# Splitting the feature fetch, splitting the second fork, and a new hand-written order in a convolution and SwiGLU kernel

## The chip, the cores and the metric

The kernel runs on one core of a Trainium2 chip. The metric is the device time of one execution in microseconds (us). Three executions of the kernel before gave 2668.44, 2670.3 and 2671.73 us; their median, 2670.3 us, is the time before. The engines are named as in the profile: PE is TensorE (its matmuls), PEld its weight loads, DVE is VectorE, ACT is ScalarE, POOL is GpSimd, and SP is SyncE, which here issues nearly all DMAs.

## The reference

A causal convolution with seven taps per head, an RMS norm, and a SwiGLU feed-forward block, all in float32:

```python
# x (8, 4096, 192), weight (8 heads, 7 taps)
w = softmax(weight, axis=-1)
out[b, s, h, g] = sum_k w[h, k] * x_pad[b, s + k, h, g]     # 6 zeros ahead of each sequence
# tokens: x = out.reshape(32768, 192)
xn = x / sqrt(mean(x * x, axis=-1) + 1e-6) * rms_g
g, val = xn @ w_gate, xn @ w_val                            # 192 -> 1536, each
return (silu(g) * val) @ w_out                              # 1536 -> 192
```

The weights come as float64 words and are converted on the chip once, at the start.

## The kernel before

**Tiling.** The 32768 tokens are handled as 32 pairs of 1024 tokens; a pair is two groups of T = 512. Pair 0 is computed by a plain method during the start of the kernel. Pairs 1 to 31 run in one loop and use fast matrix multiplication (sums of operands in place of some products), so that PE has fewer products to do and the other engines have more additions. The profile's steady state is this loop.

**One pair on PE.** A generator, `Pair.products`, gives 204 steps. Steps 0 to 119 are the products (L732): four units (`Unit`, a unit is 3 of the 12 blocks of 128 hidden features), each with the 15 entries of `CHAIN`, and each entry for the two halves h = 0 (gate, PE rows 0 to 63) and h = 1 (value, rows 64 to 127). They add into six values per half, held in the PSUM banks `ps`, of which there are four for each half. Steps 120 to 203 are the output products (L862): 42 times a wide and a slim step, in the nine runs of `OUTS`. In this text the product stage is steps 0 to 119 of a pair, the output stage is steps 120 to 203.

**Operands of the products.** `xb` holds the pair's features, six blocks of 64 x 512 (twice, for the two halves of PE's rows): x0 to x2 are group 0 and x3 to x5 are group 1. `xc` holds ten sums of them, written by `x_sum` (L655). Both have a single buffer. `XSUM` names the sums: X0 = x1 + x4, X3 = x3 + x5, X8 = x0 + x1 and X9 = x1 + x2 read `xb` alone, X1, X2, X4, X6 and X7 read `xb` and an earlier sum, X5 and X10 two earlier sums. The first products of a pair read X6 (step 0), X10 (step 2), X5 (step 6).

**The order.** `ORDER` is a hand-written string. A token `pN` lets PE's program go on by N steps; any other token is an engine letter (A = ACT, V = DVE, G = POOL, D = SP) and one action. A token with a minus belongs to the pair before. So the string fixes each engine's queue, and semaphores that the framework adds from the data fix the rest: each engine takes its queue in order. The actions that the text uses:

- `Sk.h.u` copies a PSUM bank into an SBUF tile, `C`, `D`, `R` add such a tile and a bank (DVE, L748 to L756), `G` is the SiLU (ACT, L769), `M` the product of gate and value (L776).
- `F0`, `F2`, `F3` are the forks (L693 to L697): a bank is copied into another bank, and both then go on as separate sums. `F2.h.u` copies the bank of value 4 after step 18 + h of the unit (counted from 0), and step 22 + h of the same unit adds into the bank that was copied, so it waits for the copy.
- `cvK_j` is tap K of the convolution of the pair after the next, in three parts j (tap 0 on ACT, the rest on DVE, L445); `sq`, `red`, `pow`, `bc`, `mul` are its RMS norm. 
- `S1.k` to `S4.k` are the sums of hidden blocks that the output products read (POOL, L890).
- `c1`, `s7`, `c2`, `C22`, `C21` (L908) combine the output banks X, Y, Z, and `T11` to `T22` (L877) transpose them into the output tile. `C22` reads bank X between step 179, the last one of a run of `OUTS`, and step 186, which adds into X again. The next pair's step 0 takes the bank that `T12` has read last, and its step 1 the one that `C21` has read last.
- `Dplace` writes normalised features to DRAM (`xd`), `Dfetch` reads the next pair's features back into `xb`, `Dload` loads x for the pair three on, `Dst0` and `Dst1` store the output.

`fetch` issues four DMAs of 384 KB on SP's queue, group 1 first. They may begin when the pair's last product has read `xb`.

Of the kernel before, what the change touches and what calls it, by code (L numbers as in the profile page):

```python
# [11 lines left out]
F32 = mybir.dt.float32  # L12
# [7 lines left out]
def kernel(  # L20
# [10 lines left out]
    nc = tc.nc  # L31
# [11 lines left out]
    T = 512  # L43
# [3 lines left out]
    HP = P // 2  # L47
# [10 lines left out]
    LOW, UPP = slice(0, HP), slice(HP, P)  # L58
# [29 lines left out]

    SPAN = 1509
    ORDER = (  # L90
        "p2 VT21- p2 AS40.1.0 VT11- GX4- AS40.0.0 p2 Vbc- AF0.0.0 Gmul- AF0.1.0 p2 Dst1-",
        "VC.0.0 Dst0- p2 VC.1.0 AS41.1.0 AS41.0.0 p2 AS00.1.0 AS00.0.0 p2 VD5.1.0 p2 VD5.0.0",
        "AS42.0.0 VS42.1.0 AS51.0.0 Dplace- p2 AS51.1.0 VR1.0.0 p2 VR1.1.0 VR0.0.0 p2 AF2.0.0",
        "VR0.1.0 AF2.1.0 p1 AF3.0.0 VF3.1.0 p2 AS44.0.0 p1 AG0.0.0 VR5.0.0 p1 AS44.1.0 p1",
        "GM0.1.0 VR2.0.0 p1 VR2.1.0 AG2.0.0 p2 VR5.1.0 AG4.0.0 GM2.1.0 p1 VR3.1.0 p1 AS40.0.1",
        "VR3.0.0 p1 AS40.1.1 p1 VM4.1.0 AF0.0.1 p1 AF0.1.1 p1 VC.0.1 AG3.0.0 p2 VC.1.1",
        "AS41.0.1 GM3.1.0 p1 AG5.0.0 p1 AS41.1.1 p1 GM5.1.0 VS00.1.1 AS00.0.1 p2 VD5.0.1 p1",
        "GS3.0 AS42.0.1 VD5.1.1 p1 AS42.1.1 p1 VR1.0.1 AS51.0.1 p1 GS3.1 AG1.0.0 p1 VR1.1.1",
        "AS51.1.1 p1 VR0.1.1 p1 GS1.0 AF2.0.1 p1 VR0.0.1 AF2.1.1 p1 AF3.0.1 p1 GS2.0 AF3.1.1",
        "p1 VS44.0.1 AG1.0.1 p2 AS44.1.1 VR5.0.1 GM1.1.1 p1 VR2.1.1 p1 AG5.0.1 p1 VR2.0.1 p1",  # L100
        "AG4.0.1 VR3.1.1 p1 AG0.0.1 p1 VR5.1.1 AS40.0.2 p1 GM0.1.1 VR3.0.1 p1 AS40.1.2",
        "VM4.1.1 p1 AF0.0.2 p1 GM1.1.0 AF0.1.2 VC.0.2 p1 AG3.0.1 p1 VC.1.2 p1 GM3.1.1",
        "VS41.0.2 p1 AS00.0.2 VS41.1.2 p1 AS00.1.2 p1 VM5.1.1 AG2.0.1 p1 GS1.1 VD5.0.2 p1",
        "AS42.0.2 VD5.1.2 p1 AS51.0.2 p1 GS3.2 VR1.0.2 AS42.1.2 p1 AS51.1.2 p1 VR1.1.2 p1",
        "GM2.1.1 VR0.0.2 p1 AF2.0.2 VR0.1.2 p1 AF2.1.2 p1 VF3.0.2 AG1.0.2 p1 VF3.1.2 p1",
        "GM1.1.2 AS44.0.2 p1 AG0.0.2 VR5.0.2 p1 AS44.1.2 GS1.2 p1 VR2.0.2 p1 VR2.1.2 AG2.0.2",
        "p1 GS2.1 p1 VR3.1.2 AG4.0.2 p1 VR3.0.2 p1 AS40.0.3 GM2.1.2 VR5.1.2 p1 AS40.1.3 p1",
        "VM4.1.2 AF0.0.3 p1 GM0.1.2 AG3.0.2 p1 VC.0.3 AF0.1.3 p2 VC.1.3 AG5.0.2 GM3.1.2 p1",
        "VS41.0.3 p1 AS00.0.3 VS41.1.3 p1 GM5.1.2 AS00.1.3 p1 VD5.0.3 p2 VD5.1.3 GS2.2",
        "AS42.0.3 p1 AS51.0.3 p1 VR1.0.3 AS42.1.3 GS3.3 p1 AS51.1.3 p1 VR1.1.3 p1 VR0.0.3",  # L110
        "GS3.4 p1 VF2.0.3 p1 AF2.1.3 VR0.1.3 AG0.0.3 p2 VF3.0.3 AF3.1.3 GM0.1.3 p2 AS44.1.3",
        "AS44.0.3 p1 GS1.3 p1 VR2.0.3 AG1.0.3 p1 VR2.1.3 p1 GM1.1.3 VR3.0.3 Acv0_1 p1 VR3.1.3",
        "AG3.0.3 p2 GS2.3 VR5.1.3 AG4.0.3 p2 Acv0_2 VM4.1.3 Dfetch p1 Acv0_0 p1 VM3.1.3 p1",
        "AG2.0.3 p1 GS3.5 Vcv1_1 p2 VR5.0.3 p2 GS1.4 Vcv1_2 AG5.0.3 p2 Ac1 p1 VM5.1.3 p2",
        "GS2.4 Vcv2_1 p2 Vcv2_2 p2 GS1.5 Vcv1_0 p2 Vcv3_1 p1 As7 GS4.2 p2 Vcv4_1 p2 Vcv2_0",
        "GS2.5 p2 Vcv5_1 p2 GS4.1 Vcv6_1 p2 Vcv3_0 p2 GM2.1.3 Vcv3_2 p3 Vcv4_2 p1 GS4.0 p2",
        "Vcv5_2 Ac2 p2 GX0 Vcv4_0 p2 Vcv6_2 p1 GS4.3 p1 Vcv5_0 p2 Vcv6_0 p2 VX1 p1 Asq p1 VX8",
        "p2 VX9 p1 Dload p1 VX3 p2 VC22 p2 VX6 p2 GS4.4 Vred p3 GS4.5 p4 VX5 p2 VX2 p1 VX7 p2",
        "VX10 p2 Gpow VT12 p2 VT22 p2 VC21 p1",
    )  # L120

    cst = ctx.enter_context(tc.tile_pool(name="cst", bufs=1))
# [5 lines left out]
    dram = ctx.enter_context(tc.tile_pool(name="dram", bufs=2, space=bass.MemoryType.DRAM))  # L128
# [109 lines left out]
    def load_out(i):  # L238
# [28 lines left out]
        out=taps[:], in0=w_sb[:], in1=stat[:].to_broadcast([P, H, K]), op=ALU.subtract  # L267
# [7 lines left out]
        out=taps[:], in0=taps[:], in1=ssum[:].to_broadcast([P, H, K]), op=ALU.mult  # L275
# [51 lines left out]
    xb = cst.tile([P, 2, KP, T], F32, name="xb")  # L327
# [46 lines left out]
    scr = {}  # L374
# [261 lines left out]
    def x_op(i):  # L636
        return xb[:, i // KP, i % KP, :] if i < 2 * KP else xc[:, i - 2 * KP, :]

    def fetch(p):

        if p >= PAIRS:
            return
        xd = scr.pop(p)
        for g in (1, 0):
            for rows in (LOW, UPP):
                nc.sync.dma_start(
                    out=xb[rows, g],
                    in_=xd[:, g * T : (g + 1) * T].rearrange("(k p) t -> p k t", p=HP),
                )

    def x_sum(i, eng="V"):

        d, a, b = XSUM[i]
        e = nc.gpsimd if eng == "G" else nc.vector
        e.tensor_tensor(out=xc[:, d, :], in0=x_op(a), in1=x_op(b), op=ALU.add)  # L655
# [23 lines left out]
    def put(at, do):  # L679
        heapq.heappush(line, (at, next(tick), do))  # L680
# [5 lines left out]
    def plus(s):  # L686
        return ALU.add if s > 0 else ALU.subtract
# [3 lines left out]
    def copy(eng, dst, src, s=1):  # L691
        if eng == "A":
            nc.scalar.activation(out=dst, in_=src, func=AF.Copy, scale=float(s))  # L693
        elif s < 0:
            nc.vector.tensor_scalar(out=dst, in0=src, scalar1=-1.0, scalar2=None, op0=ALU.mult)
        else:
            nc.vector.tensor_copy(out=dst, in_=src)  # L697
# [5 lines left out]
    FORK = {0: (1, 1), 2: (4, 1), 3: (5, -1)}  # L703
    RESULT = {1: ("42", -1), 0: ("41", -1), 2: ("51", -1), 5: ("44", -1), 3: ("c", 1)}

    class Unit:
        def __init__(self, u):
            self.u = u
            self.ht = None
            self.bk, self.tl = {}, {}  # L710
# [27 lines left out]
        def do(self, eng, act, h):  # L738
            tl, kind, v = self.tl, act[0], int(act[1:2] or 0)
            if kind == "S":  # L740
                t = tl[act[1:], h] = tiles.pop(0)
                copy(eng, t[:], self.old(v, h))
            elif kind == "F":
                src, s = FORK[v]
                copy(eng, self.new(v, h), self.old(src, h), s)
            elif kind == "D":
                b, t = self.old(5, h), tl.pop(("00", h))
                nc.vector.tensor_tensor(out=b, in0=b, in1=t[:], op=ALU.add)  # L748
                tiles.append(t)
            elif kind == "C":  # L750
                t = tl["c", h] = tl.pop(("40", h))
                nc.vector.tensor_tensor(out=t[:], in0=self.old(5, h), in1=t[:], op=ALU.add)
            elif kind == "R":
                k, s = RESULT[v]
                t = tl.pop((k, h))
                nc.vector.tensor_tensor(  # L756
                    out=self.hv(v) if h else t[:], in0=self.old(v, h), in1=t[:], op=plus(s)
                )
                self.leave(v, h)
                if h:  # L760
                    tiles.append(t)
                else:
                    tl["g", v] = t
            elif kind == "G":
                if v in RESULT:
                    t = src = tl["g", v]
                else:
                    t, src = tiles.pop(0), self.old(v, 0)
                nc.scalar.activation(out=t[:], in_=src[:], func=AF.Silu)  # L769
                if v not in RESULT:  # L770
                    self.leave(v, 0)
                tl["g", v] = t
            else:
                t = tl.pop(("g", v))
                src = self.hv(v) if v in RESULT else self.old(v, 1)
                engine[eng].tensor_tensor(out=self.hv(v), in0=src, in1=t[:], op=ALU.mult)  # L776
                if v not in RESULT:
                    self.leave(v, 1)
                tiles.append(t)
# [23 lines left out]
    class Pair:  # L803
# [126 lines left out]

        def ahead(self, eng, act):
            p = self.p
            if act in ("fetch", "X") or act[0] == "X":
                if p + 1 < PAIRS:
                    fetch(p + 1) if act == "fetch" else x_sum(int(act[1:]), eng)
            elif act == "load":
                load(p + 3)
            elif p + 2 < PAIRS:
                if act[0:2] == "cv":
                    part_tap(p + 2, int(act[2]), int(act[4]))  # L940
                else:
                    {
                        "sq": square, "red": reduce, "pow": factor, "bc": spread, "mul": scale,
                        "place": lambda p: done(place(p)),
                    }[act](p + 2)
# [129 lines left out]
    def done(it):  # L1075
        for _ in it:
            pass
# [27 lines left out]
    p, sl, v = plain(hts)  # L1105
# [49 lines left out]
    for p in range(1, PAIRS + 1):  # L1155
        now = Pair(p) if p < PAIRS else None
        for w in order:
# [5 lines left out]
            eng, name = w[0], w[1:]  # L1163
            of = now
            if name[-1] == "-":
                name, of = name[:-1], past
# [31 lines left out]
```

## Time and profile before

| what | value |
|---|---|
| median of three runs | 2670.3 us (2668.44 to 2671.73) |
| the profiled execution, its own time | 2670.79 us |
| its span in the profile | 2668.9 us (1.9 us lie around it) |
| granted TensorE clock | 0.998 |
| first product of pair 1, of pair 31 | 141.37 us, 2581.58 us |
| mean period of pairs 1 to 30 | (2581.58 - 141.37) / 30 = 81.34 us |
| PE, DVE, POOL, ACT busy | 98%, 88%, 74%, 59% of the span |

A busy PE is not PE at its peak: matmuls overlap, and their ends are modelled. What matters is therefore when one product starts after the one before. A group's line in the profile gives line, engine, operation, what is written and read, the shape and count, then busy time and the mean of one in ns, then idle time of the engine ahead of the group and what ended it. "issue" means that the engine waited for nothing that the profile shows.

### The profile page before, as it was taken

The numbers are of one execution on the slowest core, as the hardware profiler recorded it, in microseconds if no ns is written. First come the engines' busy times: TensorE is split into PE (matmuls) and PEld (weight loads), VectorE is DVE, ScalarE is ACT, GpSimd is POOL, SyncE is SP. The second block draws the span as 40 slices with busy tenths as digits, with TensorE's granted clock in tenths as the row PEclk, the third lists the DMA queues.
The fourth block names the chain that finished last, engine by engine and source line by source line (L and its number), as shares of the span: only waits on it lengthen the run. The fifth ranks groups of instructions, "written<-read, shape, count | busy, mean of one in ns | idle before, by whom it ended". The sixth has DMA issues, their size and how long they took to land.

```text
span 2668.9 us, 71301 instructions
## 1 busy us (share of the span) xinstructions
PE 2605.1 (98%) x29002; PEld 1761.3 (66%) x29002; DVE 2346.1 (88%) x3726; ACT 1582.4 (59%) x2933; POOL 1980.1 (74%) x1604
## 2 busy tenths in 40 slices
PE   6899999999999999999999999999999999999998
PEld 4666766666676666666666666676666667666765
DVE  8988889888899888998888998888988889988875
ACT  5375555765556755557655567655566555676554
POOL 3987778777788767787777787777876777877766
PEclk9999999999999999999999999999999999999999
DMA  6312332223321223322233322233222333222210
GB/s 141 61 38 50 62 62 38 49 38 62 62 53 39 53 43 62 62 38 49 38 62 62 57 40 49 41 62 62 42 45 43 57 62 61 38 51 38 49 37 14
DMA packets 510601, 138.03 MB, mean 52 GB/s; under 512 B 482240, under 2 KB 484800, under 8 KB 510145
## 3 DMA queue, kind: packets, MB, share of 16 engines
q1 hardware_dynamic: 509712, 133.44, 26.8%
q8 instruction: 227, 3.72, 0.6%
q14 instruction: 102, 0.84, 0.1%
q10 hardware_dynamic: 560, 0.03, 0.0%
HBM read 83.87 MB, written 49.55 MB: 50 GB/s over the span
## 4 chain that ended last, share of the span: by engine, by line
PE 85%; DVE 8%; POOL 2%; issue 2%; SPq 1%; DMA 1%; ACT 0%; DVEq 0%; POOLq 0%
PE ps L732 60%; PE ps L862 24%; DVE ps L445 3%; DVE xc L655 2%; PE ps L961 1%; DVE ht L756 1%; POOL wf L350 1%; DVE y L445 1%; DVE ht L776 0%; POOL nt L890 0%; SPq L218 0%; POOL ht L890 0%; DMA ht<-in_moe_w_val_dram 0%; SPq L1099 0%; DMA x<-in_x_dram 0%
## 5 line engine op out<-in xcount | busy, mean ns | idle before, releaser
L732 PE MATMUL ps<-xc,wf 64*128 64x512 f32 x4960 | 1304.6, 595 | 0.9 <-DVE xc L655 0.9
L732 PEld LDWEIGHTS ps<-xc,wf 64*128 64x128 f32 x4960 | 685.1, 186 | 435.4 <-issue 269.8
L732 PE MATMUL ps<-xb,wf 64*128 64x512 f32 x2480 | 744.7, 589 | 0.0
L693 ACT ACTIVATE tile<-ps 128x512 f32<-128x512 f32 (+1 forms) x744 | 421.5, 592 | 419.2 <-PE ps L732 238.5
L693 ACT ACTIVATE tls<-ps 128x512 f32<-128x512 f32 (+1 forms) x589 | 338.2, 592 | 361.0 <-PE ps L732 225.8
L776 POOL TENSOR_TENSOR ht<-ht,tile 128x512 f32<-128x512 f32 x291 | 369.5, 1276 | 235.0 <-ACT tile L769 232.7
L732 PEld LDWEIGHTS ps<-xb,wf 64*128 64x128 f32 x2480 | 359.2, 187 | 208.9 <-issue 181.9
L776 POOL TENSOR_TENSOR ht<-ht,tls 128x512 f32<-128x512 f32 x236 | 300.1, 1276 | 183.1 <-ACT tls L769 180.6
L693 ACT ACTIVATE ps<-ps 128x512 f32<-128x512 f32 x620 | 338.1, 581 | 72.1 <-PE ps L732 69.5
L890 POOL TENSOR_TENSOR early<-ht 128x512 f32<-128x512 f32 x279 | 361.8, 1311 | 9.5 <-DVE ht L776 6.9
L862 PE MATMUL ps<-ht,wo_sb 128*32 128x256 f32 (+1 forms) x6944 | 316.9, 326 | 19.0 <-issue 15.6
L445 DVE SCALAR_TENSOR_TENSOR ps<-xh,tp,ps 128x512 f32<-128x512 f32 x435 | 307.7, 749 | 3.1
L862 PEld LDWEIGHTS ps<-ht,wo_sb 128*32 128x32 f32 x6944 | 232.0, 110 | 104.7 <-issue 25.2
L756 DVE TENSOR_TENSOR tile<-ps,tile 128x512 f32<-128x512 f32 x344 | 233.5, 684 | 38.0 <-PE ps L732 20.8
L890 POOL TENSOR_TENSOR ht<-ht 128x512 f32<-128x512 f32 x186 | 251.8, 1354 | 2.4
L862 PE MATMUL ps<-ht,x 128*32 128x128 f32 (+1 forms) x5952 | 251.5, 326 | 0.0
L862 PEld LDWEIGHTS ps<-ht,x 128*32 128x32 f32 x5952 | 221.0, 110 | 24.8
L756 DVE TENSOR_TENSOR ht<-ps,tile 128x512 f32<-128x512 f32 x347 | 232.9, 681 | 1.7
L769 ACT ACTIVATE tile<-tile 128x512 f32<-128x512 f32 x344 | 214.9, 625 | 32.8 <-DVE tile L756 32.8
L756 DVE TENSOR_TENSOR tls<-ps,tls 128x512 f32<-128x512 f32 x276 | 187.5, 684 | 32.8 <-PE ps L732 19.2
L862 PE MATMUL ps<-early,x 128*32 128x256 f32 (+1 forms) x4464 | 198.9, 326 | 5.5 <-issue 5.5
L769 ACT ACTIVATE tls<-tls 128x512 f32<-128x512 f32 x276 | 172.5, 625 | 25.5 <-DVE tls L756 25.5
(129 smaller groups left out, 3163.8 us busy)
## 6 DMA issues: line engine op xcount, KB each, us to landing
xb<-xd SPq DMA_DIRECT2D x124, 384.0 KB
xd<-yn SPq DMA_DIRECT2D x248, 96.0 KB
out_dram<-o_sb SPq DMA_DIRECT2D x186, 128.0 KB
xh<-in_x_dram SPq DMA_DIRECT2D x192, 105.0 KB
xh<-in_x_dram SPq DMA_DIRECT2D x56, 98.4 KB
ht<-in_moe_w_gate_dram SPq DMA_DIRECT2D x12, 192.0 KB
ht<-in_moe_w_val_dram SPq DMA_DIRECT2D x12, 192.0 KB
tls<-in_moe_w_out_dram SPq DMA_DIRECT2D x8, 192.0 KB
```

Of the source, the lines that this page charges most:

```text
L350: nc.gpsimd.tensor_tensor(out=t[:, d, :], in0=t[:, a, :], in1=t[:, b, :], op=ALU.add if op == "add" else ALU.subtract,)
L445: nc.vector.scalar_tensor_tensor(out=dst, in0=xk, scalar=w, in1=at, op0=ALU.mult, op1=ALU.add)
L655: e.tensor_tensor(out=xc[:, d, :], in0=x_op(a), in1=x_op(b), op=ALU.add)
L693: nc.scalar.activation(out=dst, in_=src, func=AF.Copy, scale=float(s))
L732: nc.tensor.matmul(out=self.new(v, h, True) if first else self.old(v, h), lhsT=wf[self.u][HALF[h], WAT[i], :], rhs=x_op(XOP[i])[HALF[h]], ...
L756: nc.vector.tensor_tensor(out=self.hv(v) if h else t[:], in0=self.old(v, h), in1=t[:], op=plus(s))
L769: nc.scalar.activation(out=t[:], in_=src[:], func=AF.Silu)
L776: engine[eng].tensor_tensor(out=self.hv(v), in0=src, in1=t[:], op=ALU.mult)
L862: nc.tensor.matmul(out=self.bank(b)[i * Q : (i + 1) * Q, at : at + n], lhsT=left, rhs=cols, start=fresh, stop=True, skip_group_check=True, ...
L890: engine[eng].tensor_tensor(out=dst, in0=a, in1=b, op=op)
L961: nc.tensor.matmul(out=bank(h, bks[h])[:], lhsT=wf[u][HALF[h], k * NF + f, :], rhs=xb[HALF[h], g, k, :], start=(k == 0), stop=(k == KP - 1 ...
```

## The change

`Dfetch` becomes two tokens. `fetA` fetches group 1 (two DMAs of 384 KB). `fetB` first issues a DMA of one 4-byte word out of what `fetA` has written, into a DRAM tile `mark`, and then fetches group 0 (two DMAs). The one-word DMA reads what the second DMA of `fetA` writes, so SP waits for that DMA to land before it issues it, and the DMAs of group 0 stand behind it in SP's queue.

`Dload` moves from step 178 of its pair to step 8 of the next one, behind the two stores.

The second fork is cut at column 320: ACT copies columns 0 to 319 (`F2a`), DVE columns 320 to 511 (`F2b`), for all eight of a pair. Before, seven of the eight were on ACT, and one (`F2.0.3`) on DVE, each over 512 columns. In the built program, each `F2b` waits for its `F2a` (they write the same bank), and PE's step waits for `F2b`.

`ORDER` is new. Per pair, the actions by engine:

| engine | before | after |
|---|---|---|
| ACT | 7 F2, 4 F3, 41 S | 8 F2a, 5 F3, 39 S |
| DVE | 1 F2, 4 F3, 7 S, 7 M, 9 X | 8 F2b, 3 F3, 9 S, 6 M, 4 X (X0, X1, X3, X8) |
| POOL | 17 M, 24 sums S1 to S4, 2 X (X0, X4) | 18 M, 24 sums, 7 X (X2, X4, X5, X6, X7, X9, X10) |

X7 and X4 run at steps 6 and 8 of the next pair. PE's products and their order are the same.

```diff
@@ ORDER, the last rows of each
-        "AG3.0.3 p2 GS2.3 VR5.1.3 AG4.0.3 p2 Acv0_2 VM4.1.3 Dfetch p1 Acv0_0 p1 VM3.1.3 p1",
-        "AG2.0.3 p1 GS3.5 Vcv1_1 p2 VR5.0.3 p2 GS1.4 Vcv1_2 AG5.0.3 p2 Ac1 p1 VM5.1.3 p2",
-        "GS2.4 Vcv2_1 p2 Vcv2_2 p2 GS1.5 Vcv1_0 p2 Vcv3_1 p1 As7 GS4.2 p2 Vcv4_1 p2 Vcv2_0",
-        "GS2.5 p2 Vcv5_1 p2 GS4.1 Vcv6_1 p2 Vcv3_0 p2 GM2.1.3 Vcv3_2 p3 Vcv4_2 p1 GS4.0 p2",
-        "Vcv5_2 Ac2 p2 GX0 Vcv4_0 p2 Vcv6_2 p1 GS4.3 p1 Vcv5_0 p2 Vcv6_0 p2 VX1 p1 Asq p1 VX8",
-        "p2 VX9 p1 Dload p1 VX3 p2 VC22 p2 VX6 p2 GS4.4 Vred p3 GS4.5 p4 VX5 p2 VX2 p1 VX7 p2",
-        "VX10 p2 Gpow VT12 p2 VT22 p2 VC21 p1",
+        "p2 AS44.0.3 AS44.1.3 p1 VR5.0.3 GS3.4 p1 VR2.0.3 p1 AG5.0.3 p1 VR5.1.3 GS2.3 AG4.0.3",
+        "p2 Acv0_2 VM4.1.3 p1 AG0.0.3 p1 VR3.0.3 p1 GS3.5 DfetA p1 VR3.1.3 AG3.0.3 p1 Vcv1_2",
+        "p1 Acv0_1 p1 GM3.1.3 AG2.0.3 VR2.1.3 p2 Acv0_0 p2 GS1.4 Ac1 Vcv1_0 p3 VM0.1.3 p2",
+        "VM5.1.3 p2 Vcv1_1 p1 GS1.5 p2 Vcv2_1 p2 Vcv2_2 GS2.5 As7 DfetB p2 Vcv2_0 p2 GS2.4",
+        "Vcv3_1 p2 Vcv3_2 p2 VX3 p2 GS4.3 Vcv4_1 p2 Vcv5_1 p2 GS4.4 Vcv3_0 p2 Vcv4_2 p1 GS4.0",
+        "p1 Ac2 Vcv4_0 p2 Vcv6_1 p1 GM2.1.3 p4 VX0 p1 GS4.5 Vcv5_0 p3 Vcv6_0 p1 GS4.1 p1",
+        "Vcv5_2 p3 Vcv6_2 GX9 p2 VC22 Asq p2 VX1 p2 GX2 VT22 p2 Vred p2 GX6 p3 GX5 p1 VC21 p3",
+        "VX8 p2 GX10 VT21 p2 VT12 p1 Gpow p3",
...
+    mark = dram.tile([1, 2], F32, name="mark")
+
+    def fetch_part(p, act):
+        xd, g = scr[p], int(act == "fetA")
+        if g == 0:
+            nc.sync.dma_start(out=mark[:, 0:1], in_=xb[HP : HP + 1, 1, 0, 0:1])
+            scr.pop(p)
+        for rows in (LOW, UPP):
+            nc.sync.dma_start(
+                out=xb[rows, g],
+                in_=xd[:, g * T : (g + 1) * T].rearrange("(k p) t -> p k t", p=HP),
+            )
...
+    CUT = 320
...
             elif kind == "F":
                 src, s = FORK[v]
-                copy(eng, self.new(v, h), self.old(src, h), s)
+                cols = {"a": slice(0, CUT), "b": slice(CUT, T)}.get(act[2:], slice(0, T))
+                dst = self.old(v, h) if (v, h) in self.bk else self.new(v, h)
+                copy(eng, dst[:, cols], self.old(src, h)[:, cols], s)
```

## The prediction

> **What bounds the kernel now.** First the page's busy shares and its chain of waits:
>
> ```profile
> PE 2605.1 (98%) x29002; PEld 1761.3 (66%) x29002; DVE 2346.1 (88%) x3726; ACT 1582.4 (59%) x2933; POOL 1980.1 (74%) x1604
> ...
> PE 85%; DVE 8%; POOL 2%; issue 2%; SPq 1%; DMA 1%; ACT 0%; DVEq 0%; POOLq 0%
> ```
>
> PE bounds nearly everything, so only what PE waits for can be won. Next the stretches of one quiet pair (its output stage, then all of it) and of the longest pair; columns: length, then busy time of PE, PEld, DVE, ACT, POOL.
>
> ```profile
> 684.16:712.14 27.98, 27.65 (x674) 20.52 (x673) 27.63 (x42) 6.58 (x11) 22.42 (x20) 1.00 0.54 90
> 631.25:712.14 80.89, 80.56 (x917) 53.08 (x913) 72.46 (x117) 49.35 (x91) 60.96 (x49) 1.00 0.28 52
> 387.05:469.76 82.71, 80.32 (x915) 52.21 (x912) 73.55 (x117) 49.16 (x91) 61.21 (x49) 1.00 0.27 50
> ```
>
> In the quiet pair's output stage DVE is busy 27.63 of 27.98 us: it is full. Without any wait PE starts a chain entry every 0.8585 us (60 entries: 51.51) and an output block every 0.65 (42: 27.3, with 0.17 at the borders 27.47). So 78.98 of the mean period of 81.34 us is work, and 2.36 us is waiting, of three kinds.
>
> *Instructions.* PE's timeline in the long pair, then the DMA queues in two stretches (441 to 448 us, then 448 to 450), then two groups of the page:
>
> ```profile
> 447.36 1.26 PE L862 MATMUL ps<-ht,wo_sb 128*32 128x256 f32 x23
> 451.01 1.16 PE L862 MATMUL ps<-ht,wo_sb 128*32 128x256 f32 x24 [2.39 <-issue]
> ```
> ```profile
> q1 hardware_dynamic: 800, 1.54, 97.0%
> ...
> q1 hardware_dynamic: 30, 0.03, 9.9%
> q8 instruction: 1, 0.02, 4.3%
> ```
> ```profile
> L862 PE MATMUL ps<-ht,wo_sb 128*32 128x256 f32 (+1 forms) x6944 | 316.9, 326 | 19.0 <-issue 15.6
> L862 PE MATMUL ps<-early,x 128*32 128x256 f32 (+1 forms) x4464 | 198.9, 326 | 5.5 <-issue 5.5
> ```
>
> PE stops with nothing to wait for, while the fetch of the features fills the DMA engines; the next block of PE's instructions moves only when the fetch has drained, and PE goes on 1.5 us later. Blocks come every 256 PE instructions (one per 5.2 us in the output stage). The groups give 15.6 + 5.5 = 21.1 us for the kernel, 0.69 per pair.
>
> *DVE's tail.* DVE's timeline at the end of the quiet pair, and PE's and PEld's beside it:
>
> ```profile
> 700.97 1.68 DVE L655 TENSOR_TENSOR xc<-xb,xc 128x512 f32<-128x512 f32 x1
> 702.57 2.97 DVE L655 TENSOR_TENSOR xc<-xb 128x512 f32<-128x512 f32 x3
> 705.46 0.55 DVE L908 TENSOR_TENSOR tls<-ps,tls 128x384 f32<-128x384 f32 x1
> ...
> 712.21 0.51 DVE L908 TENSOR_TENSOR tls<-ps,tls 128x384 f32<-128x384 f32 x1
> ```
> ```profile
> 706.15 1.51 PE L862 MATMUL ps<-ht,wo_sb 128*32 128x256 f32 x32 [0.33 <-DVE tls L908]
> ```
> ```profile
> 680.45 0.38 PEld L732 LDWEIGHTS ps<-xc,wf 64*128 64x128 f32 x4 [0.56 <-DVE ps L697]
> ...
> 712.78 0.72 PEld L732 LDWEIGHTS ps<-xc,wf 64*128 64x128 f32 x5 [0.35 <-DVE tls L908]
> ```
>
> C22 (705.46) comes late behind the X sums: PE loses 0.51 us by its starts. C21 (712.21) is last of all, and the next pair's step 1 waits for it: 0.52. The adds stretch beside POOL: X1 1.68 us, X8 1.77, against 0.68 alone. Pairs that lost time to instructions have neither wait, since DVE caught up: that is why the quiet pairs still take 80.9.
>
> *The second fork.* At 680.45 PE waits for `F2.0.3`; by PE's starts the four units lose 0.14, 0.08, 0.08 and 0.42: 0.71 per pair, in every pair.
>
> **The change, part by part.** E is the end of a product stage.
>
> *Split fetch.* The 1.5 MB take 7.6 us. A block asked for after all four DMAs were issued waited up to 5.4 us, and PE stopped where the wait was over about 3.2. In halves of 3.8 us, with at least SP's issue (0.65 each) and the landing between them, the longest wait should be some 3 us. I take 0.05 for the 0.69 per pair; both ends: 0 and 0.69, and I stay near the first because requests that found only two DMAs queued waited 1.2 to 2.9 us. The Trainium skill ("DMA: Bandwidth & Descriptors", Queues, rings and completion order) says that a DMA engine takes turns between queues, packet by packet. By that rule an instruction block would never wait for a whole fetch, and the split would win nothing; the empty q8 row above disagrees. The one word costs SP one issue; behind it stand only the two DMAs of group 0. They land near E + 11.5 instead of E + 8.5; the readers X0 and X9 are due after E + 16, so it is covered; without cover it would cost 3.
>
> *Load later.* Eight issues, 7.2 us of SP, now behind the stores at the next pair's step 8; the first reader is at step 122, 45 us on: nothing. `Dplace` stands behind it, at step 26, 100 steps before its reader: nothing.
>
> *Fork.* Before, two copies of 0.58 in a row on ACT. After: F2a 0.42 (between 0.584 for 512 columns and 0.473 for 384), wake of DVE 0.03, F2b 0.36 (DVE: 0.68 for 512, 0.53 for 384), one after the other, since F2b waits. The bank is ready 1.0 to 1.06 us after step 18 starts, and PE wants it 1.72 after: 1.03 + 0.42 + 0.03 + 0.36 + 0.06 = 1.90, so PE loses 0.19 in each unit, 0.76 in all against 0.71. A 192-column copy is not in the trace: at 0.27 (the 128-column transpose) it loses 0.10 a unit, at 0.53 0.36. Behind the waiting F2b on DVE stands R0, which has room. This part is worth about nothing: -0.05, ends +0.3 and -0.75.
>
> *POOL.* 2 to 7 X sums and 17 to 18 M: 6 x 1.27 = 7.6 us more, 61 to 69 of some 80. In the output stage 18 operations of 1.27 us end near E + 26; X6 (due E + 27.5) and X10 (0.9 later) make it with one to three us over. Nothing, if it holds.
>
> *DVE's tail.* Up to cv1_0 waits for ACT set the time: E + 4.55. Then cv1_0 0.70, M0 and M5 1.30, 16 taps at 0.70 11.2, X3 and X0 1.22: C22 starts at E + 19.0. C22 0.47, X1 0.61, T22 0.57, red 2.2, C21 0.47, X8 0.61, T21 0.57: T12 ends at E + 25.1 (with its 0.60). PE needs T12 at E + 27.4. That leaves 2.3 us for what six adds out of SBUF (M0, M5, X3, X0, X1, X8) lose beside POOL. Rows for it: 0 (M3, where POOL lost 0.33), 0.33 (M5), 1.0 and 1.09 (X1, X8), mean 0.6, six times 3.6. Laying POOL's queue beside DVE's by these durations I find 0.1, 0, 0.95, 0.6, 0.35, 0.35 = 2.35, because POOL waits for M5 itself. I take a slip of 0.3 us (ends: 0, and 3.7 at 1.0 each). The Trainium skill ("SBUF — State Buffer", Who interferes with whom) says that a DVE add with two SBUF inputs and a reading GpSimd instruction exclude each other whole: the later one waits to the other's end. It speaks against moving sums to POOL beside DVE's own, and would allow up to one POOL operation per add.
>
> *Sum.* Product stage 51.51 + 0.10 (first step) + 0.76 + 0.17 (last) = 52.54; output stage 27.47 + 0.05 + 0.3 = 27.8; period 80.35 against 81.34. 30 periods x 0.99 = 30 us. From the profiled execution's 2670.8 that is 2641; the median is 0.5 lower: 2640.5.
>
> **The rivals.**
> - *The port decides (slower).* POOL is busy through nearly the whole output stage, and each add waits long. The point from which it decides is 81.34 - 52.54 - 25.1 = 3.7 us over six adds, 0.6 each, which is the mean of the rows. At 0.95 each T12 ends at E + 30.8, the period is 83.3, and the time 2670 + 30 x 2.0 = 2730; at 0.75 2693. For it: X1 and X8 lost 1.0 and more. Against: the laid-out queue, and POOL's own waits.
> - *The stalls stay.* If a half fetch holds the block as long as a whole one, 0.64 per pair comes back: 2660. For it: waits of 3.5 us already stop PE. Against: the requests early in a burst.
> - *All waits fall.* No slip, and the fork costs 0.3 less: 79.7 per pair, 2621. For it: C21 now stands well ahead of the end. Against: F2b waits for F2a.
>
> **How the numbers follow.** The forecast (2627 to 2656) has 0.5, all waits fall 0.1, stalls stay 0.14, the port 0.2, and 0.06 is for other waits that a new order can bring. The range 2620 to 2680 leaves out about 0.06 below and 0.13 above. A measurement of this kernel can tell about 0.2% (5.3 us) from no change. Faster: 0.5 + 0.1 + 0.10 of the stalls = 0.70; same: 0.10; slower: 0.20.
>
> **What would show it.** Right: no idle "issue" of over a microsecond on L862; q8 packets between two bursts of xb; PE waiting some 0.2 us at F2b in each unit; T12 the last DVE action before a pair, and a wait of a few tenths on it. DVE's output stage should be idle for about 2 us, and POOL near 90%. Wrong: X3, X0, X1, X8 of 1.7 us each, PE waiting for C22 or T12 by a microsecond; a wait of PE for an X sum on POOL, or of X0 for a late group 0.

## The result and the profile after

The changed kernel takes 2666.7 us (median of 4 runs, 2665.5 to 2669.1) against 2669.8 us for the kernel before on the same chip: ratio 0.9989, interval 0.9972 to 1.0006. That is no change that can be told from none. The forecast was 2640.5 us. The profiled execution took 2665.5 us with a span of 2663.6.

The page's busy shares and its chain of waits:

```profile
PE 2623.9 (99%) x29002; PEld 1594.7 (60%) x29002; DVE 2321.4 (87%) x3793; ACT 1562.4 (59%) x2933; POOL 2188.7 (82%) x1785
...
PE 94%; DVE 2%; POOL 1%; DMA 1%; SPq 1%; issue 1%; ACT 1%; DVEq 0%; POOLq 0%
```

"issue" in the chain fell from 2 to 1%, DVE from 8 to 2%, and PE's records now cover 99% of the span. Yet the span is only 5 us shorter: a matmul that waits for one half of the array while the other half runs shows PE as busy.

The same quiet pair (pair 7: its product stage, its output stage, all of it; busy time of PE, PEld, DVE, ACT, POOL):

```profile
631.82:685.26 53.44, 53.39 (x243) 27.72 (x242) 45.99 (x79) 42.02 (x81) 41.82 (x33) 1.00 0.26 44
685.26:712.69 27.43, 27.43 (x673) 20.05 (x672) 25.87 (x39) 6.72 (x11) 24.84 (x20) 1.00 0.27 61
631.82:712.69 80.87, 80.82 (x914) 47.77 (x912) 71.86 (x118) 48.74 (x91) 66.66 (x52) 1.00 0.27 49
```

The output stage has lost its waits: 27.43 us, which is work and borders alone, where it had 27.98. The product stage has grown from 52.92 to 53.44, and 52.54 had been forecast. The two nearly cancel: a quiet pair takes 80.87 instead of 80.89.

An entry is one product for each half of the array: the lower half (h = 0), then the upper one (h = 1). Each of these float32 matmuls leaves two records; the second starts 0.43 us after the first, or 0.53 after a wait. The wait of the last product entry lies between it and the first output matmul. By the starts of the lower half's matmuls, averaged over 30 pairs (us per pair beyond the undisturbed rate):

| wait | before | after | forecast |
|---|---|---|---|
| first entries of a pair | 0.34 | 0.16 | 0.10 |
| second fork, four units | 0.71 | 1.31 | 0.76 |
| last product entry | 0.19 | 0.54 | 0.17 |
| blocks of instructions | 0.86 | 0.20 | 0.05 |
| C22 | 0.20 | 0 | 0 |
| T12's slip | 0 | 0 | 0.30 |
| borders of the output stage | 0.22 | 0.17 | 0.17 |
| sum | 2.52 | 2.38 | 1.55 |

The split fetch and the new order gained about as much as was forecast; the fork and the last entry took it back. The forecast is short by 0.83 us per pair, 25 us in 30.

One fork in unit 0 of pair 7, rows of the timeline:

```profile
640.70 0.75 ACT L707 ACTIVATE ps<-ps 128x320 f32<-128x320 f32 x2 [0.45 <-PE ps L748]
641.15 0.70 DVE L711 COPY ps<-ps 128x192 f32<-128x192 f32 x2 [0.56 <-ACT ps L707]
641.58 1.48 PEld L748 LDWEIGHTS ps<-xc,wf 64*128 64x128 f32 x8 [0.88 <-DVE ps L711]
```

The two F2a run on ACT, each F2b behind its F2a on DVE, and PE's next weights wait 0.88 us for DVE. In unit 1 the upper half is behind already, and PE waits for the two F2b one after the other:

```profile
654.77 0.29 PEld L748 LDWEIGHTS ps<-xc,wf 64*128 64x128 f32 x2 [0.41 <-DVE ps L711]
655.24 0.29 PEld L748 LDWEIGHTS ps<-xc,wf 64*128 64x128 f32 x3 [0.18 <-DVE ps L711]
```

### The profile page after: what moved, and what is told of

The parts are those of the page before. It is cut to its first block, busy times and chain, and to the rows that moved or that the text cites. A ratio compares the mean times of both kernels' runs of the same rounds, so it can differ in the third digit from the quotient of the medians.

```text
span 2663.6 us, 71444 instructions
## 1 busy us (share of the span) xinstructions
PE 2623.9 (99%) x29002; PEld 1594.7 (60%) x29002; DVE 2321.4 (87%) x3793; ACT 1562.4 (59%) x2933; POOL 2188.7 (82%) x1785
## 4 chain that ended last, share of the span: by engine, by line
PE 94%; DVE 2%; POOL 1%; DMA 1%; SPq 1%; issue 1%; ACT 1%; DVEq 0%; POOLq 0%
PE ps L748 61%; PE ps L880 32%; PE ps L979 1%; POOL wf L351 1%; ACT ps L707 0%; DVE ps L711 0%; SPq L219 0%; SPq L1117 0%; DMA x<-in_x_dram 0%; DMA xh<-in_x_dram 0%; POOL wo_sb L313 0%; DMA ht<-in_moe_w_gate_dram 0%; DMA ht<-in_moe_w_val_dram 0%; DVE xc L669 0%; DVE ht L996 0%
## 5 line engine op out<-in xcount | busy, mean ns | idle before, releaser
L748 PEld LDWEIGHTS ps<-xc,wf 64*128 64x128 f32 x4960 | 619.2, 186 | 547.8 <-issue 376.2
L707 ACT ACTIVATE tile<-ps 128x512 f32<-128x512 f32 (+1 forms) x703 | 396.4, 593 | 339.9 <-PE ps L748 194.6
L794 POOL TENSOR_TENSOR ht<-ht,tile 128x512 f32<-128x512 f32 x310 | 391.7, 1274 | 110.5 <-ACT tile L787 110.5
L748 PEld LDWEIGHTS ps<-xb,wf 64*128 64x128 f32 x2480 | 319.8, 187 | 232.2 <-issue 192.7
L794 POOL TENSOR_TENSOR ht<-ht,tls 128x512 f32<-128x512 f32 x248 | 314.3, 1274 | 95.8 <-ACT tls L787 95.8
L908 POOL TENSOR_TENSOR ht<-ht 128x512 f32<-128x512 f32 x186 | 238.4, 1282 | 49.1 <-DVE ht L794 36.9
L880 PEld LDWEIGHTS ps<-ht,wo_sb 128*32 128x32 f32 x6944 | 218.0, 110 | 91.2 <-issue 23.5
L880 PE MATMUL ps<-ht,x 128*32 128x256 f32 (+1 forms) x5952 | 249.6, 326 | 0.2 <-issue 0.2
L880 PEld LDWEIGHTS ps<-ht,x 128*32 128x32 f32 x5952 | 194.4, 110 | 49.6 <-issue 0.3
L774 DVE TENSOR_TENSOR ht<-ps,tls 128x512 f32<-128x512 f32 x263 | 177.9, 681 | 8.2 <-ACT tls L707 8.2
```

The source lines that it names most:

```text
L748: nc.tensor.matmul(out=self.new(v, h, True) if first else self.old(v, h), lhsT=wf[self.u][HALF[h], WAT[i], :], rhs=x_op(XOP[i])[HALF[h]], ...
L774: nc.vector.tensor_tensor(out=self.hv(v) if h else t[:], in0=self.old(v, h), in1=t[:], op=plus(s))
L880: nc.tensor.matmul(out=self.bank(b)[i * Q : (i + 1) * Q, at : at + n], lhsT=left, rhs=cols, start=fresh, stop=True, skip_group_check=True, ...
L908: engine[eng].tensor_tensor(out=dst, in0=a, in1=b, op=op)
```

## The experiments

All are compared with runs of the kernel before on their own chip; a few microseconds lie between chips.

**e1: the second fork whole again.**

```
-  AF2a.0.u VF2b.0.u ... AF2a.1.u VF2b.1.u        (u = 0 to 3)
+  AF2.0.u ... AF2.1.u
```

> The changed kernel with the second fork whole on ScalarE again (F2 in one copy, no F2b), nothing else moved. Theory (the fork in two parts is a chain of four actions that ends too late, and it holds R0.0.3 on VectorE): the changed kernel loses 0.32 to 0.35 us at the fork of each unit, 1.31 per pair, and 0.52 at the last product entry; with whole copies the fork should lose 0.08 to 0.14 per unit as in the kernel before (0.38 per pair) and the last entry 0.17. Gain 0.93 + 0.35 = 1.28 us per pair, 38 us: 2628. Rival 1 (the last entry waits for ScalarE's own queue, not for R0.0.3): only 0.93 per pair, 2639. Rival 2 (what the product stage wins is given back in the output stage, because VectorE's tail ends there at its limit): 2655 to 2667, with PE waiting for T12.

Measured: 2638.9 us, ratio 0.9877 (0.9863 to 0.9891). The forks lose 0.37 us per pair (0.09, 0.09, 0.10, 0.09), the last entry 0.58. The same fork in its timeline:

```profile
633.26 1.07 ACT L707 ACTIVATE ps<-ps 128x512 f32<-128x512 f32 x2 [0.45 <-PE ps L748]
...
633.89 0.29 PEld L748 LDWEIGHTS ps<-xc,wf 64*128 64x128 f32 x2 [0.64 <-ACT ps L707]
```

Two whole copies on one engine end after 1.07 us; the four parts on two engines ended 1.15 us after the first began (640.70 to 641.85). The wait is 0.64 in place of 0.88, since the lower half's bank is copied after 0.58 us in place of 0.82. So the part of the change that was put down as "worth about nothing" costs 28 to 30 us in this order, and it alone hides the rest. Rival 1's number (2639) came true, not my theory's: the last entry has another cause than R0.0.3.

**e2: R0.0.3 ahead of F2b in the fourth unit.**

```
-  AG1.0.3 VR0.1.3 p1 AF2a.0.3 ... VF2b.1.3 p1 VR0.0.3
+  AG1.0.3 VR0.0.3 p1 AF2a.0.3 ... VF2b.1.3 p1 VR0.1.3
```

> The changed kernel with R0.0.3 and R0.1.3 exchanged in the fourth unit, so that the result which frees the bank of F3.0.3 stands ahead of F2b. Theory (F3.0.3 on ScalarE waits for R0.0.3, which stands behind F2b.1.3 on VectorE, and S44.0.3 and S44.1.3 come late behind it): the last product entry loses 0.17 instead of 0.52 us, 0.35 per pair, 10 us: 2656; the forks unchanged. Rival (ScalarE's queue is late there for another reason): 2667, the entry still at 0.52.

Measured: 2668.2 us, ratio 0.9987 (0.9978 to 0.9996), the last entry at 0.55. The theory on R0.0.3 falls.

**e11: one copy of the kernel before moved.** After e2 the trace showed what the last entry counts. The two matmuls of an entry, lower half and upper half, are queued in turn. In the changed kernel the upper half starts a pair 0.01 us behind the lower, falls 0.33 behind at the first fork, where its copy is the second one, is 0.47 behind at the end of that unit, and stays near there (0.45 at the end of the stage); the output stage needs both, so by this theory the lag is paid at the last entry. In the kernel before the lag is 0.49, but F2.0.3 on VectorE held up the lower half by 0.41 more than the other forks did, and that brought the two level (lag 0.08). (The 0.37 and 0.32 of the expectation come from another pairing of a matmul's two records; paired by their distance the lag is 0.49.)

```
-  VF2.0.3 p1 AF2.1.3
+  AF2.0.3 p1 AF2.1.3
```

> The kernel before with one copy moved: F2.0.3, the lower half of the fork in the fourth unit, on ScalarE in place of VectorE. Theory (the upper half of the array runs 0.37 us behind the lower from the first fork on; in the fourth unit the late copy on VectorE holds up the lower half by 0.32, which only brings the two level, and without it the same is paid at the last product entry): the fork loses 0.09 in place of 0.42, the last entry 0.52 in place of 0.19, and the time stays: 2670. Rival (the 0.42 of the fourth unit is a loss like any other): 0.33 per pair, 10 us less: 2660.

Measured: 2668.1 us, ratio 0.9985 (0.9976 to 0.9994). The fourth fork now loses 0.08 in place of 0.49; 0.12 is lost ahead of that unit's last product instead, and the last entry loses 0.47 in place of 0.19: the same wait at other places. The product stage as a whole takes 52.74 us in place of 52.75. The remaining gain of 0.1 us per pair is spread over the waits of the output stage.

**e6: the split fork alone, in the kernel before.**

```
-  AF2.0.u ... AF2.1.u                            (VF2.0.3 in unit 3)
+  AF2a.0.u VF2b.0.u ... AF2a.1.u VF2b.1.u
```

> The kernel before with the fork alone changed: each copy of F2 in two parts, ScalarE then VectorE, at the places of the whole copies. Theory (the second part can only start when the first has ended, so each bank is ready later than by one whole copy, and the two halves of the array end apart): PE loses about 0.32 us at the fork of each unit, and the later half adds 0.3 at the last product entry; product stage 0.5 to 0.9 us longer, 15 to 27 us: 2684 to 2696. Rival (the forecast's sum: the part is worth nothing): 2666 to 2670.

Measured: 2723.6 us, ratio 1.0193 (1.0179 to 1.0207): the sign is the theory's, the size twice it. DVE's and PEld's timelines in unit 0 of pair 7 show why:

```profile
653.39 0.37 DVE L697 COPY ps<-ps 128x192 f32<-128x192 f32 x1
653.67 0.68 DVE L760 TENSOR_TENSOR ht<-ps,tls 128x512 f32<-128x512 f32 x1
654.27 0.35 DVE L697 COPY ps<-ps 128x192 f32<-128x192 f32 x1
```
```profile
653.81 0.29 PEld L734 LDWEIGHTS ps<-xc,wf 64*128 64x128 f32 x2 [0.66 <-DVE ps L697]
654.68 0.30 PEld L734 LDWEIGHTS ps<-xc,wf 64*128 64x128 f32 x4 [0.57 <-DVE ps L697]
```

In the old order R0.1.0 stands on DVE between the two F2b, so the upper half's bank comes another 0.6 us later. The upper half falls 0.86 behind, a whole entry, and the four forks lose 0.33, 0.67, 0.38 and 0.79. The changed order keeps R0 out of there: it belongs to the split.

**e7: lower copy on ScalarE, upper copy on VectorE, both whole.**

```
-  AF2a.0.u VF2b.0.u ... AF2a.1.u VF2b.1.u
+  AF2.0.u ... VF2.1.u
```

> The changed kernel with whole copies at the second fork, that of the lower half on ScalarE and that of the upper half on VectorE, side by side. Theory (the product stage is set by the later of the two halves of the array, and a fork costs what its copies come late in each half): ScalarE's copy is ready 1.70 us after step 18 and wanted at 1.72, no loss; VectorE's loses some 0.06 per unit in the upper half and 0.2 once, where R0.0 is still running; waits of the product stage 1.9 -> 0.7 us, 1.2 per pair, 36 us against the changed kernel: 2631, and the last entry falls from 0.52 to 0.3 or less. Rival (the later half does not matter, only the loss of the lower half): 1.3 us per pair and the last entry still at 0.52: the waits end at 0.62 + 0.35, 2640.

Measured: 2644.6 us, ratio 0.9900 (0.9886 to 0.9913). The forks lose 0.57 per pair, 0.31 of it in the fourth unit, and the last entry is still 0.53: by the timelines R0 on DVE, and from the second unit on F3.1 too, put the upper half behind again (0.31 after the first unit, 0.45 at the end). The expectation of 2631 was a miss; two copies side by side are no better than two in a row while DVE has other work there.

**e3 and e5: the fetch.** e3 puts the changed kernel's whole fetch at one place; e5 gives the kernel before the two parts.

```
e3:  if g == 0: scr.pop(p); return
     for g in (1, 0): for rows in (LOW, UPP): nc.sync.dma_start(...)
e5:  -  Dfetch ... As7 GS4.2
     +  DfetA ... As7 DfetB GS4.2          (fetch_part as in the change)
```

> The changed kernel with the whole fetch (all four DMAs) at the place of its first part and no one-word DMA. Theory (the halves shorten what a block of PE's instructions waits): waits of instructions in the output stage go from 0.23 us per pair back to the 0.69 of the kernel before, 0.46 per pair, 14 us: 2681, with idle of one to two and a half microseconds on the output matmuls in about half of the pairs. Rival (the split does nothing, the fewer waits come from where the blocks fall by chance): 2667.

> The kernel before with the fetch alone changed: two parts, the one-word DMA between them, the second part at the place of s7. Theory (the split removes most waits for instructions, but the kernel before has VectorE's tail behind them: pairs that lose no time to instructions wait for C22 and C21 instead): the period falls from 81.34 us to the quiet pairs' 80.9 plus what is left of the waits for instructions (0.1 to 0.25), 6 to 12 us less: 2658 to 2664. Rival (the tail does not come back): the whole difference between one fetch and two in the changed kernel, 0.65 us per pair, 20 us: 2650.

Measured: e3 2686.4 us, ratio 1.0054 (1.0039 to 1.0068); e5 2663.6 us, ratio 0.9970 (0.9958 to 0.9981). The groups of the output matmuls with idle time in e3, and two of e5's:

```profile
L881 PE MATMUL ps<-ht,wo_sb 128*32 128x256 f32 (+1 forms) x6944 | 319.3, 326 | 16.0 <-issue 16.0
L881 PE MATMUL ps<-early,x 128*32 128x256 f32 (+1 forms) x4464 | 199.4, 326 | 3.9 <-issue 3.8
```
```profile
L875 PE MATMUL ps<-ht,wo_sb 128*32 128x256 f32 (+1 forms) x6944 | 309.2, 327 | 7.1 <-DVE tile L921 4.1 <-DVE tls L921 2.7
L875 PE MATMUL ps<-nt,x 128*32 128x256 f32 (+1 forms) x1488 | 68.6, 326 | 4.4 <-issue 4.3
```

With one fetch the waits for instructions are back (0.84 us per pair, as before the change). In e5 they fall from 0.86 to 0.28, but PE now waits for C22 in most pairs (0.40 in place of 0.20) and at a pair's first entries (0.51 in place of 0.34): of 0.58 saved, 0.37 is given back to DVE's tail. In the changed order, where that tail is gone, the same split is worth 0.7 us per pair, 17 to 20 us.

**e4: four parts.**

```
 for rows in (LOW, UPP):
+    if rows == UPP:
+        nc.sync.dma_start(out=mark[:, 1:2], in_=xb[0:1, g, 0, 0:1])
```

> The changed kernel with a one-word DMA between all four DMAs of the fetch. Theory (a block waits as long as one burst holds the engines, and PE stops over about 3.2 us of waiting; a quarter lasts 2 us): no PE idle for instructions, 0.23 us per pair less, 7 us: 2660. The last quarter should land near E + 15.7, just ahead of X0 at E + 16. Rival 1 (X0 and with it T12 come late behind the last quarter): 0.5 to 2 us per pair more, 2675 to 2720. Rival 2 (bursts of any length hold the block): 2667.

Measured: 2703.2 us, ratio 1.0116 (1.0101 to 1.0130): rival 1. In pair 7, DVE, then PE:

```profile
711.21 0.69 DVE L671 TENSOR_TENSOR xc<-xb 128x512 f32<-128x512 f32 x1 [3.94 <-DMA xb<-xd]
```
```profile
715.41 2.79 PE L882 MATMUL ps<-ht,wo_sb 128*32 128x256 f32 x32 [2.50 <-DVE tile L928]
```

X0 waits for the last quarter, C22 stands behind X0, PE waits for C22. Where X0 ended only 1.2 us later than in the changed kernel, PE already lost 0.7. The quarters seem to have ended PE's stops for instructions: in its waits no idle time of the output matmuls is put down to "issue" any more. But PE waits for C22 in nearly every pair here, which could cover a late block; e8 and e9, with quarters in this stage, have neither stop.

**e8 and e9: the fetch begun inside the product stage.** Group 0 is not read after step 107, so it can be fetched before the stage ends (in e8's pair 7 5.8 us before); group 1 follows in two parts, X3 two taps later. e8 does this on e7, e9 on e1.

```
-  DfetA at step 125, DfetB at step 145
+  DfetB at step 110 (group 0), DfetA at step 125 (group 1: one word, LOW, one word, UPP)
```

> The kernel e7 with the fetch arranged anew: group 0 at step 109, inside the product stage, where PE uses up its instructions slowly; group 1 at the end of the product stage in two DMAs with a one-word DMA between; X3 two taps later. Theory (a block of instructions may wait about 3.2 us in the output stage, and a burst of 2 us leaves it that): no PE idle for instructions, 0.25 us per pair less than e7, 7 us, 2624. Rival (X3 waits for the last quarter and T12 comes late, as X0 did in e4): 0.5 us per pair more, 2645.

> The two cures together: the second fork whole on ScalarE as in e1, the fetch with an early group 0 and two parts of group 1 as in e8. Theory (the two waits are independent of each other): e1's mean period 80.27 us less its 0.22 us of waits for instructions, 80.05, 7 us less than e1: 2632. Rival (a new wait for X3 or T12 appears as the product stage shortens): 2636 to 2645.

Measured: e8 2636.0 us, ratio 0.9867 (0.9852 to 0.9882); e9 2631.2 us, ratio 0.9845 (0.9832 to 0.9859), the fastest here: some 41 us below the kernel before on its chip. Its chain of waits and its output matmuls:

```profile
PE 96%; DVE 1%; DMA 1%; SPq 1%; issue 0%; POOL 0%; ACT 0%; DVEq 0%; POOLq 0%
```
```profile
L882 PE MATMUL ps<-ht,wo_sb 128*32 128x256 f32 (+1 forms) x6944 | 305.6, 326 | 0.0
L882 PE MATMUL ps<-early,x 128*32 128x256 f32 (+1 forms) x4464 | 192.7, 326 | 0.0
```

No output matmul waits for instructions, and every output stage holds only its 0.14 us of borders.

**e10: the loads at their old place.**

```
-  p2 VC.0.0 Dload-
+  VX1 p1 Dload p1 GX2         (step 184; 178 in the kernel before)
```

> The changed kernel with the eight loads of the tokens issued where the kernel before issues them, in the output stage (step 186). Prediction and theory: the loads' place is worth nothing, 2667 within noise. Rival (the loads beside the stores had delayed the fetches or the instructions): more than 5 us slower.

Measured: 2675.5 us, ratio 1.0011 (1.0002 to 1.0020), against 0.9989 for the changed kernel; the mean period is 81.48 instead of 81.19, 9 us in 30. The rival's size came true, but by another cause. After every fourth pair PE starts the next pair over a microsecond late. POOL, DVE and PE in pair 9:

```profile
871.15 0.21 POOL L150 MEMSET xh<- 8x144 f32 x1 [0.63 <-issue]
871.34 2.52 POOL L669 TENSOR_TENSOR xc<-xb,xc 128x512 f32<-128x512 f32 x2
```
```profile
871.43 2.98 DVE L669 TENSOR_TENSOR xc<-xb,xc 128x512 f32<-128x512 f32 x1
```
```profile
879.41 1.99 PE L748 MATMUL ps<-xc,wf 64*128 64x512 f32 x8 [1.23 <-DVE o_sb L895]
```

A load at the start of a sequence (every fourth pair) issues a memset on POOL, and it starts only when DVE's last tap, a reader of the tokens, has ended (at 871.0; in all seven such pairs the tap ends 0.1 us before the memset). X2, queued behind it, starts 0.8 us later than in the other pairs and so 0.1 us before DVE's X1. X1 then lasts 2.98 us instead of 0.89, until POOL's X2 and X6 are over, and T12 comes late. In the seven pairs X1 took 2.97 to 2.98 five times, 2.80 and 1.89; in most others, where it starts 0.94 after POOL's X2, 0.88 to 0.90. The prediction counted the load's eight DMAs and not its memset: "Load later: nothing" holds only because the load did move.

## Why the prediction failed

**The fork: the step that failed.** The term was 0.19 us a unit, 0.76 in all, from the chain F2a, wake, F2b in the lower half: bank ready for PE at 1.90 us after step 18, wanted at 1.72 (its terms give 0.18). It measured 0.32 to 0.33 a unit, 1.31 in all. The chain itself came out nearly as forecast: in unit 1 of pair 7 F2a starts 1.06 after step 18, F2b (0.37, forecast 0.36) ends at 1.87, and PE starts at 1.93, 0.21 late. What the sum put at nothing is the 0.10 that PE loses behind such a wait: the weights are loaded 0.00 us ahead of the matmul in place of 0.43, and its first record lasts 0.69 in place of 0.59. The sum had these 0.10 at a pair's first step, but not at the forks. In units 1 to 3 the upper half loses the same 0.21 and 0.10 on its own F2b.

The comparison with the old fork was wrong too. In e1 a whole copy in the lower half ends at 1.64, the weights are loaded at 1.69, and PE starts at 1.72: just in time, with a loss of 0.08 because the load stands only 0.03 ahead. Three of the old forks lose the same 0.08. So nothing was left for a longer chain. Splitting a copy over two engines shortens it only if the parts run together; here both write one bank and the second waits for the first's semaphore, so 0.42 + 0.03 + 0.37 = 0.82 stands in place of 0.58. The 0.24 between them, four times, is 0.96 per pair, 29 us; e1 wins back 0.94 at the forks.

**The last entry.** 0.17 was taken as a fixed border. It is 0.09 plus the lag of the upper half: 0.54 with a lag of 0.45 in the changed kernel, 0.58 with 0.49 in e1, 0.47 with 0.38 in e11, 0.19 with 0.10 before. The lag was small before only because of the late F2.0.3 (e11), so the 0.42 of the fourth unit and the 0.17 had to be read together: of what that fork lost, all but 0.08 was no loss that a new fork could save. Against the true cost of the old forks (0.3 per pair and a lag of 0.49) the split was a loss from the start, not "-0.05".

**The waits for instructions: mostly right.** They fell by 0.66 (0.64 forecast, from idle time in place of starts). "The longest wait should be some 3 us" is wrong, though: in pair 6 the block was asked for some 0.8 us before the second half's data (group 0) began to move, an estimate from the count of PE's instructions, and got through after it, some 4.7 us later. The DMA queues of that half, then of the 1.5 us behind it, and PE:

```profile
q1 hardware_dynamic: 402, 0.77, 93.1%
```
```profile
q8 instruction: 1, 0.02, 5.5%
q1 hardware_dynamic: 10, 0.00, 1.9%
```
```profile
616.74 1.28 PE L880 MATMUL ps<-nt,x 128*32 128x256 f32 x24 [1.07 <-issue]
```

That no block moved while 402 feature packets did speaks once more against turns by packet.

**DVE's tail: no slip, partly by luck.** T12 ends at 712.24, 27.0 us after E, and PE is through with its work at E + 27.4: no slip. POOL is busy for 24.84 of 27.43 us, the 90% forecast. The sums beside it, DVE and POOL (X3, X0, X1, X8; then S4.3, S4.4):

```profile
695.43 1.75 DVE L669 TENSOR_TENSOR xc<-xb 128x512 f32<-128x512 f32 x1
701.18 1.52 DVE L669 TENSOR_TENSOR xc<-xb 128x512 f32<-128x512 f32 x1
705.99 0.89 DVE L669 TENSOR_TENSOR xc<-xb,xc 128x512 f32<-128x512 f32 x1
709.97 1.19 DVE L669 TENSOR_TENSOR xc<-xb 128x512 f32<-128x512 f32 x1
```
```profile
695.35 1.29 POOL L908 TENSOR_TENSOR more<-ht,nt 128x512 f32<-128x512 f32 x1
696.59 1.73 POOL L908 TENSOR_TENSOR tls<-ht,nt 128x512 f32<-128x512 f32 x1
```

Over 0.68 each they lose 1.07, 0.84, 0.21 and 0.51, with M0's 0.18 and M5's 0 together 2.8 us, against 2.35 laid out and 3.7 at which the port would have decided. So the adds lost more than was laid out, and T12 came early all the same because the rest of the sum was 0.9 us too long: E + 27.0 less 2.8 is 24.2, where the forecast had 25.1. cv1_0 starts at E + 4.05 in place of 4.55, and a tap takes 0.68 in place of 0.70. X3 starts with S4.3 and gets through when that ends; S4.4 then waits for X3. The Trainium skill ("SBUF — State Buffer", Who interferes with whom) says that such a pair excludes each other whole, and this row agrees. In e10's 2.98 the add on DVE waited for two on POOL, one more than the prediction allowed; why two there and one here, no run shows.

**The rivals.** The port did not decide; e10 shows how near it stood. The stalls did not stay (0.20 is left of 0.86). "All waits fall" had the forks lower than the sum, and they came higher. The prediction asked what would be late next for DVE's tail, but not for the two halves of the array.

## What to carry to other kernels

Where an engine takes two interleaved streams, follow the later stream through every wait, and ask where its lag is paid: a wait that one stream loses may only bring the two level. Price a wait with what stands behind it (here 0.08 to 0.10, where the weights were loaded only just ahead). Splitting an operation between two engines is a loss while both parts write one buffer whose semaphore puts them in a row and the whole operation was just in time; compare the end of the last part with the end of the last whole copy. A transfer that starves the instruction queue is best moved to a stage in which instructions are used up slowly.

## What was not expected of the hardware

One add on DVE took 2.98 us where it began 0.1 us after an add on POOL, and 0.89 where it began 0.94 after it: when an add starts can matter more than how many adds there are. And PE counts as 99% busy in a kernel that can still be made 35 us faster: a matmul that waits in one half of the array does not show as idle time.
